# Whole-array products of a fused attention and MLP kernel issued as four products of 32 columns, with one scheduling policy for the whole run

## The chip, the cores and the metric

The kernel runs on one core of one Trainium2 chip. The metric is the device time of one execution, in microseconds (us). The core has a matrix engine (PE, with its weight loads shown apart as PEld), a vector engine (DVE), a scalar engine that evaluates functions (ACT), a general engine (POOL) and a queue engine (SP) that issues most transfers. PE writes its products to PSUM, a memory of 8 banks of 128 partitions by 512 numbers; only ACT and DVE read it here.

## What is computed

A block of 2048 tokens of width 512 goes through a layer norm, and then through two branches that are added to the input:

```
xn = layernorm(x)
A  = softmax(q k^T / 4) v, 32 heads of width 16, then @ wo      (q, k, v = xn @ wqkv)
h  = layernorm(xn)
u  = gelu(h^T @ w1 + b1)        512 x 1376
y  = (u @ w2 + b2)^T            2048 x 512
out = x + A + y
```

The attention is the bulk: 32 heads of 2048 x 2048 scores, each score exponentiated once. All inputs and the output are bfloat16.

## The kernel before

**Blocks and groups.** The scores are cut in 32 blocks (4 blocks of 512 queries times 8 sets of 4 heads), and each block in 16 groups of 128 keys: 512 groups. A group holds 4 heads, and so 4 products K*Q of 32 rows each (line 663; a head's width of 16 is padded to 32), one for each quarter of the rows of the array. Each gives 128 keys by 512 queries in one PSUM bank.

**Two ways to exponentiate.** A group goes either to ACT or to DVE. On ACT (line 686), two instructions take two banks each (128x1024). On DVE, four first passes (line 746, or 754 for two banks at once) turn the scores into 16-bit integers whose bits are read as bfloat16, a rough exponential; two more "planes" are made from the result by adding a constant (line 759 on DVE, line 766 on POOL), and the three planes together approximate the exponential. So a group given to ACT costs four P*V products, one given to DVE twelve.

**P*V.** Line 699 multiplies the exponentials with V. Four products stand side by side, each with 128 rows and 32 columns of the array (16 columns of V, a column of ones for the denominator, padding), and each writes 32 partitions of the same PSUM bank, number 6. These four are called a quad below.

**Whole-array products.** Everything else on PE uses all 128 rows and columns in one product: the transposes of the normalised input (line 781), the projections to Q, K and V (line 604), the two products of the MLP (lines 1016 and 1047), the output projection (lines 1057 and 1065), sums that are carried through the identity (line 1095), and fillers of zeros (lines 826 and 1797). Transposes and part of the projections have 128 moving columns, the others 512. They accumulate in banks 4, 5 and 7.

**Who sets the order.** All instructions are laid out by a planner inside the kernel when it is built (class Sched, line 170 on, and the functions from line 1300 on). It keeps a clock for each engine, adds each instruction with a duration (`occ`) and a delay to its result (`lat`), and at each step asks for PE (pe_step, line 1724, and pe_fill, line 1649), DVE (dve_step, line 1846), POOL and SP (misc_step, line 1904) what to issue next. On PE it chooses between scores for ACT, scores for DVE, P*V and whole-array products. It knows three forms of the array, called S (scores), P (P*V) and F (whole array), and charges SWITCH = 95 ns (line 166) when the form changes. The choice between ACT and DVE for a group falls out of this, as does every queue's order; once built, each engine runs its list in order and waits on semaphores.

**Policies.** Sixteen numbers steer the choices: how long to wait for scores, how to rank P*V against whole-array products, when DVE takes groups, and so on. POLICY (line 97) holds 66 such tuples, one for each 10 us of the planned time, and line 1940 changes to the next.

**Denominators.** At a block's end its result is copied from PSUM, the denominators are gathered through DRAM by SP's transfers, inverted on DVE (line 1283), broadcast by four transfers, and multiplied in on POOL (line 1305). LAT_I and LAT_B (line 445) are the delays that the planner assumes for the second gathering and the broadcast.

**Constants.** The function late_consts (line 515) sets up the output weights and b1h (line 526), the bias of the MLP in single precision, a cast of 128x11 numbers that is read when the first MLP product is evacuated (line 1027).

Of the kernel before, what the change touches and what calls it, by code (L numbers as in the profile page):

```python
# [15 lines left out]
S = 2048  # L16
# [3 lines left out]
F = 1376  # L20
# [46 lines left out]
class Op:  # L67
# [29 lines left out]
POLICY = [  # L97
    (160.0, 150.0, 400.0, -1, 0, 1300.0, 0.0, 0.05, 2, 3, 2, 7500.0, 0, 0.0, 1000.0, 1),
    (115.0, 150.0, 300.0, -1, 0, 900.0, 100.0, 0.05, 2, 5, 2, 8000.0, 84539, 150.0, 1000.0, 1),
    (135.0, 160.0, 250.0, -1, 0, 1300.0, 0.0, 0.0, 3, 2, 2, 7500.0, 73548, 0.0, 1000.0, 1),  # L100
    (135.0, 160.0, 250.0, -1, 0, 1300.0, 0.0, 0.0, 3, 2, 2, 7500.0, 73548, 0.0, 1000.0, 1),
    (135.0, 160.0, 250.0, -1, 0, 1300.0, 0.0, 0.0, 3, 2, 2, 7500.0, 73548, 0.0, 1000.0, 1),
    (180.0, 80.0, 400.0, -1, 0, 1300.0, 0.0, 0.1, 2, 3, 2, 5500.0, 43264, 0.0, 700.0, 2),
    (160.0, 150.0, 400.0, -1, 0, 1300.0, 0.0, 0.05, 2, 3, 2, 7500.0, 0, 0.0, 1000.0, 1),
    (240.0, 150.0, 500.0, -1, 1, 1300.0, 0.0, 0.05, 1, 4, 0.9, 5500.0, 84839, 0.0, 1000.0, 1),
    (225.0, 140.0, 400.0, 1, 1, 1300.0, 200.0, 0.05, 1, 5, 2, 8500.0, 76820, 0.0, 800.0, 1),
    (205.0, 160.0, 350.0, -1, 0, 900.0, 0.0, 0.05, 1, 3, 2, 8500.0, 36251, 0.0, 800.0, 1),
    (130.0, 80.0, 200.0, -1, 0, 900.0, 100.0, 0.2, 2, 3, 2, 10500.0, 47584, 0.0, 900.0, 0),
    (140.0, 70.0, 400.0, 1, 1, 2000.0, 0.0, 0.05, 3, 5, 2, 8500.0, 0, 0.0, 1100.0, 1),
    (230.0, 70.0, 400.0, 1, 0, 900.0, 0.0, 0.05, 3, 5, 2, 8000.0, 41963, 1.0, 700.0, 1),  # L110
    (160.0, 150.0, 400.0, -1, 0, 1300.0, 0.0, 0.05, 2, 3, 2, 7500.0, 0, 0.0, 1000.0, 1),
    (160.0, 150.0, 400.0, -1, 0, 1300.0, 0.0, 0.05, 2, 3, 2, 7500.0, 0, 0.0, 1000.0, 1),
    (210.0, 120.0, 550.0, -1, 0, 1300.0, 0.0, 0.05, 2, 3, 0.9, 8000.0, 0, 0.0, 1000.0, 1),
    (180.0, 210.0, 550.0, 1, 0, 900.0, 100.0, 0.05, 1, 5, 2, 10500.0, 0, 0.0, 1100.0, 1),
    (160.0, 190.0, 400.0, 1, 0, 2000.0, 0.0, 0.1, 1, 2, 2, 5500.0, 0, 150.0, 1100.0, 0),
    (230.0, 170.0, 500.0, 1, 1, 2000.0, 100.0, 0.0, 1, 3, 2, 7500.0, 34273, 150.0, 1000.0, 2),
    (230.0, 140.0, 350.0, -1, 0, 1300.0, 0.0, 0.1, 3, 5, 2, 7500.0, 64300, 0.0, 1100.0, 2),
    (230.0, 140.0, 350.0, -1, 0, 1300.0, 0.0, 0.1, 3, 5, 2, 7500.0, 64300, 0.0, 1100.0, 2),
    (160.0, 150.0, 400.0, -1, 0, 1300.0, 0.0, 0.05, 2, 3, 2, 7500.0, 0, 0.0, 1000.0, 1),
    (125.0, 120.0, 500.0, 1, 1, 900.0, 0.0, 0.2, 3, 4, 0.9, 8500.0, 53346, 0.0, 800.0, 1),  # L120
    (125.0, 120.0, 500.0, 1, 1, 900.0, 0.0, 0.2, 3, 4, 0.9, 8500.0, 53346, 0.0, 800.0, 1),
    (225.0, 150.0, 300.0, -1, 0, 1300.0, 200.0, 0.1, 2, 4, 0.9, 10500.0, 77244, 0.0, 1100.0, 1),
    (165.0, 200.0, 550.0, -1, 1, 1300.0, 0.0, 0.1, 2, 4, 2, 7000.0, 7520, 0.0, 1200.0, 1),
    (160.0, 150.0, 400.0, -1, 0, 1300.0, 0.0, 0.05, 2, 3, 2, 7500.0, 0, 0.0, 1000.0, 1),
    (160.0, 150.0, 400.0, -1, 0, 1300.0, 0.0, 0.05, 2, 3, 2, 7500.0, 0, 0.0, 1000.0, 1),
    (120.0, 140.0, 550.0, -1, 0, 1300.0, 0.0, 0.1, 3, 3, 2, 5500.0, 0, 0.0, 1000.0, 0),
    (120.0, 140.0, 550.0, -1, 0, 1300.0, 0.0, 0.1, 3, 3, 2, 5500.0, 0, 0.0, 1000.0, 0),
    (235.0, 90.0, 550.0, 1, 1, 1300.0, 100.0, 0.05, 3, 3, 0.9, 8000.0, 37810, 0.0, 1100.0, 0),
    (120.0, 240.0, 350.0, -1, 0, 2000.0, 0.0, 0.05, 2, 4, 2, 10500.0, 56289, 0.0, 500.0, 1),
    (160.0, 100.0, 550.0, -1, 1, 2000.0, 0.0, 0.2, 3, 5, 2, 9500.0, 62766, 0.0, 500.0, 0),  # L130
    (130.0, 210.0, 200.0, -1, 0, 1300.0, 0.0, 0.05, 2, 3, 2, 5500.0, 42813, 1.0, 700.0, 1),
    (130.0, 210.0, 200.0, -1, 0, 1300.0, 0.0, 0.05, 2, 3, 2, 5500.0, 42813, 1.0, 700.0, 1),
    (185.0, 110.0, 550.0, -1, 0, 2000.0, 0.0, 0.2, 2, 4, 2, 8000.0, 0, 0.0, 700.0, 1),
    (145.0, 90.0, 300.0, 1, 0, 1300.0, 100.0, 0.05, 2, 2, 0.9, 7000.0, 71587, 0.0, 900.0, 1),
    (175.0, 190.0, 450.0, -1, 0, 2000.0, 200.0, 0.0, 1, 3, 2, 7500.0, 15056, 0.0, 500.0, 2),
    (130.0, 160.0, 400.0, -1, 0, 1300.0, 0.0, 0.05, 2, 5, 0.9, 7000.0, 0, 0.0, 1100.0, 1),
    (180.0, 190.0, 450.0, 1, 0, 1300.0, 0.0, 0.0, 1, 2, 2, 7500.0, 49636, 0.0, 1000.0, 1),
    (205.0, 230.0, 300.0, -1, 0, 1300.0, 200.0, 0.1, 1, 2, 2, 10500.0, 0, 0.0, 1000.0, 2),
    (160.0, 150.0, 400.0, -1, 0, 1300.0, 0.0, 0.05, 2, 3, 2, 7500.0, 0, 0.0, 1000.0, 1),
    (125.0, 140.0, 400.0, -1, 1, 1300.0, 0.0, 0.2, 2, 3, 2, 9500.0, 77989, 0.0, 500.0, 2),  # L140
    (205.0, 180.0, 200.0, -1, 1, 1300.0, 100.0, 0.05, 2, 5, 2, 7500.0, 0, 1.0, 1800.0, 1),
    (170.0, 120.0, 350.0, -1, 0, 1300.0, 0.0, 0.05, 1, 3, 2, 7500.0, 96514, 0.0, 900.0, 2),
    (215.0, 190.0, 250.0, -1, 1, 900.0, 0.0, 0.2, 3, 5, 2, 5500.0, 0, 1.0, 1400.0, 2),
    (120.0, 100.0, 400.0, 1, 0, 1300.0, 200.0, 0.2, 1, 3, 0.9, 10500.0, 26863, 0.0, 500.0, 1),
    (180.0, 240.0, 400.0, -1, 0, 2000.0, 200.0, 0.05, 2, 2, 2, 8500.0, 81850, 0.0, 1800.0, 2),
    (195.0, 140.0, 300.0, 1, 1, 1300.0, 100.0, 0.05, 3, 5, 0.9, 6500.0, 0, 1.0, 1800.0, 0),
    (110.0, 70.0, 500.0, -1, 0, 1300.0, 0.0, 0.2, 2, 3, 2, 7500.0, 0, 0.0, 1100.0, 0),
    (190.0, 230.0, 400.0, -1, 1, 2000.0, 0.0, 0.1, 2, 3, 2, 7000.0, 97277, 0.0, 1400.0, 1),
    (115.0, 120.0, 550.0, -1, 0, 900.0, 100.0, 0.0, 3, 3, 2, 8000.0, 76554, 0.0, 1400.0, 1),
    (145.0, 80.0, 450.0, -1, 0, 900.0, 0.0, 0.05, 3, 3, 2, 7500.0, 0, 0.0, 700.0, 1),  # L150
    (115.0, 190.0, 350.0, -1, 0, 900.0, 0.0, 0.1, 2, 3, 2, 8000.0, 14865, 1.0, 1100.0, 1),
    (140.0, 60.0, 400.0, -1, 0, 900.0, 100.0, 0.0, 1, 5, 0.9, 7500.0, 65796, 150.0, 1000.0, 0),
    (185.0, 220.0, 500.0, 1, 0, 2000.0, 100.0, 0.1, 2, 2, 0.9, 7500.0, 0, 0.0, 500.0, 1),
    (115.0, 180.0, 550.0, -1, 0, 1300.0, 0.0, 0.05, 3, 5, 2, 9500.0, 57145, 150.0, 1000.0, 0),
    (115.0, 230.0, 350.0, -1, 1, 1300.0, 100.0, 0.0, 2, 4, 2, 5500.0, 49062, 0.0, 900.0, 2),
# [185 lines left out]
def bass_parallel_sum__softmax_full_mha__mixer_token_mlp__prompt_kernel(  # L341
# [18 lines left out]
    with ExitStack() as es:  # L360
# [81 lines left out]

        NPRE = 4
        TABLE = 1283.0
        LAT_I, LAT_B = 3500.0, 3000.0


        sc.add("pool", lambda e: e.memset(ident[:], 0.0), writes=[("ident",)], occ=200, lat=430)
# [1647 lines left out]
```

## Time and profile before

| what | us |
|---|---|
| median of 3 runs | 665.76 (663.84 to 665.94) |
| profiled execution | 664.15 |
| its span, first to last instruction | 662.4 |
| PE busy / weight loads busy | 650.1 / 191.4 |
| ACT busy | 648.7 |
| DVE busy | 614.1 |
| POOL busy | 416.2 |
| mean granted clock of PE | 0.996 |

Busy time of PE and ACT counts an instruction from its start to its (modelled) end, and instructions of one engine overlap, so a busy engine may still wait a little. The prices in the text that follows are therefore taken from the start of one instruction to the start of the next. A line with "x4" in a timeline stands for four instructions merged, with the time from the start of the first to the end of the last. "Idle before, releaser" is time in which an engine did nothing, and what ended it. The chain of work that ended last is followed back from the last instruction: at each step to what released it, or to the instruction before it on its engine.

### The profile page before, as it was taken

The numbers are of one execution on the slowest core, as the hardware profiler recorded it, in microseconds if no ns is written. First come the engines' busy times: TensorE is split into PE (matmuls) and PEld (weight loads), VectorE is DVE, ScalarE is ACT, GpSimd is POOL, SyncE is SP. The second block draws the span as 40 slices with busy tenths as digits, with TensorE's granted clock in tenths as the row PEclk, the third lists the DMA queues.
The fourth block names the chain that finished last, engine by engine and source line by source line (L and its number), as shares of the span: only waits on it lengthen the run. The fifth ranks groups of instructions, "written<-read, shape, count | busy, mean of one in ns | idle before, by whom it ended". The sixth has DMA issues, their size and how long they took to land.

```text
span 662.4 us, 15718 instructions
## 1 busy us (share of the span) xinstructions
PE 650.1 (98%) x6387; PEld 191.4 (29%) x6387; DVE 614.1 (93%) x1059; ACT 648.7 (98%) x709; POOL 416.2 (63%) x287
## 2 busy tenths in 40 slices
PE   8999999999999999999999999999999999999997
PEld 4533333322222222222222222222222222222222
DVE  7888999999999999999998999999999998989995
ACT  7989999999999999999999999999999999999996
POOL 5640585664754664665768667697578657596731
PEclk9989999999999999999999999999999999999999
DMA  7025100022022222220012211212110221312011
GB/s 223 2 65 93 35 14 19 23 57 52 15 49 61 52 54 57 50 39 18 22 38 58 74 49 43 64 46 64 34 43 20 52 55 35 89 50 51 26 31 49
DMA packets 78368, 32.67 MB, mean 49 GB/s; under 512 B 63004, under 2 KB 74204, under 8 KB 78296
## 3 DMA queue, kind: packets, MB, share of 16 engines
q1 hardware_dynamic: 77864, 31.27, 19.3%
q8 instruction: 50, 0.82, 0.5%
q10 hardware_dynamic: 432, 0.39, 0.2%
q14 instruction: 22, 0.18, 0.1%
HBM read 26.08 MB, written 2.61 MB: 43 GB/s over the span
## 4 chain that ended last, share of the span: by engine, by line
PE 72%; ACT 21%; DVE 4%; DMA 1%; SPq 1%; POOL 0%; issue 0%; DVEq 0%; POOLq 0%
PE ps L663 26%; PE ps L699 26%; ACT pT L686 21%; PE ps L1016 7%; PE ps L604 6%; PE ps L1047 5%; PE ps L1057 2%; SPq L435 1%; PE ps L781 1%; DMA den_s<-den_scr 0%; DVE plx L746 0%; DVE wqkv_sb L746 0%; DMA x_sb<-in_A_x_dram 0%; DVE h_sb L590 0%; ACT QT L624 0%
## 5 line engine op out<-in xcount | busy, mean ns | idle before, releaser
L686 ACT ACTIVATE pT<-ps 128x1024 bf16<-128x1024 f32 x685 | 630.4, 1133 | 3.2 <-PE ps L663 3.0
L663 PE MATMUL ps<-QT,KT 32*128 32x512 bf16 x2048 | 279.4, 385 | 4.9 <-ACT pT L686 2.9
L663 PEld LDWEIGHTS ps<-QT,KT 32*128 32x128 bf16 x2048 | 71.5, 91 | 269.2 <-ACT pT L686 247.6
L699 PE MATMUL ps<-pT,V 128*32 128x512 bf16 x1370 | 129.4, 390 | 0.3 <-DVE OT L1268 0.3
L746 DVE TENSOR_SCALAR x_sb<-ps 128x512 int16<-128x512 f32 x174 | 115.5, 684 | 7.1 <-PE ps L663 6.2
L746 DVE TENSOR_SCALAR xn_sb<-ps 128x512 int16<-128x512 f32 x156 | 102.5, 683 | 6.2 <-PE ps L663 5.5
L746 DVE TENSOR_SCALAR plx<-ps 128x512 int16<-128x512 f32 x106 | 70.2, 684 | 7.6 <-PE ps L663 6.8
L746 DVE TENSOR_SCALAR wqkv_sb<-ps 128x512 int16<-128x512 f32 x78 | 51.3, 684 | 3.9 <-PE ps L663 3.5
L1016 PE MATMUL ps<-h_sb,w1blk 128*128 128x512 bf16 (+1 forms) x176 | 54.0, 386 | 0.0
L1047 PE MATMUL ps<-gT,w2blk 128*128 128x512 bf16 (+1 forms) x176 | 53.7, 385 | 0.0
L699 PEld LDWEIGHTS ps<-pT,V 128*32 128x32 bf16 x1370 | 32.2, 94 | 67.5 <-issue 63.5
L746 DVE TENSOR_SCALAR xnT<-ps 128x512 int16<-128x512 f32 x64 | 41.9, 682 | 1.9 <-PE ps L663 1.5
L604 PE MATMUL ps<-xnT,wqkv_sb 128*128 128x512 bf16 (+1 forms) x188 | 40.9, 316 | 0.3
L766 POOL TENSOR_TENSOR plx<-xn_sb,shift_w 128x1024 int32<-128x1024 int32 x12 | 22.7, 1891 | 25.4 <-DVE x_sb L759 20.7
L766 POOL TENSOR_TENSOR xn_sb<-x_sb,shift_w 128x1024 int32<-128x1024 int32 x15 | 28.3, 1891 | 15.4 <-DVE xn_sb L759 7.3
L699 PE MATMUL ps<-x_sb,V 128*32 128x512 bf16 x372 | 36.1, 382 | 0.2 <-DVE OT L1268 0.2
L766 POOL TENSOR_TENSOR x_sb<-plx,shift_w 128x1024 int32<-128x1024 int32 x13 | 24.5, 1891 | 13.4 <-DVE x_sb L759 12.1
L746 DVE TENSOR_SCALAR w1blk<-ps 128x512 int16<-128x512 f32 x46 | 30.6, 684 | 1.8 <-PE ps L663 1.3
L766 POOL TENSOR_TENSOR x_sb<-xn_sb,shift_w 128x1024 int32<-128x1024 int32 x12 | 22.7, 1891 | 14.4 <-DVE xnT L759 8.2
L699 PE MATMUL ps<-xn_sb,V 128*32 128x512 bf16 x318 | 30.5, 382 | 0.0
L1305 POOL TENSOR_TENSOR oT<-OT,denb 128x512 bf16<-128x512 f32 x16 | 20.3, 1271 | 14.6 <-DMA denb<-rec_scr 9.2
L1305 POOL TENSOR_TENSOR otmp<-OT,denb 128x512 bf16<-128x512 f32 x15 | 19.1, 1271 | 16.3 <-DVE x_sb L759 10.8
(190 smaller groups left out, 857.9 us busy)
## 6 DMA issues: line engine op xcount, KB each, us to landing
denb<-rec_scr SPq DMA_DIRECT2D x124, 64.0 KB, 2.0
w1blk<-in_B_w_dram SPq DMA_DIRECT2D x10, 512.0 KB, 5.3
w2blk<-in_B_w_dram SPq DMA_DIRECT2D x16, 320.0 KB, 3.7
xres<-in_A_x_dram SPq DMA_DIRECT2D x16, 128.0 KB, 2.2
QT<-qst SPq DMA_DIRECT2D x120, 16.0 KB, 1.8
out_dram<-osb SPq DMA_DIRECT2D x14, 128.0 KB, 1.7
wqkv_sb<-in_A_wqkv_dram SPq DMA_DIRECT2D x3, 384.0 KB, 8.8
x_sb<-in_A_x_dram SPq DMA_DIRECT2D x2, 512.0 KB, 7.8
```

Source lines behind the costliest of these rows:

```text
L435: return eng.dma_start(dst, src)
L604: return sc.add("pe", lambda e: e.matmul(dst, lhsT=lhsT, rhs=rhs, start=(ct == 0), stop=(ct == NCT - 1)), reads=reads, writes=[("bank", bk ...
L663: return sc.add("pe", lambda e: e.matmul(bank(bk), lhsT=KT[32 * r:32 * r + 32, T, 128 * kt:128 * (kt + 1)], rhs=QT[32 * r:32 * r + 32, slo ...
L686: return sc.add("act", lambda e: e.activation(pT_buf(buf), ps[:, slot * 1024:(slot + 1) * 1024], ACTF.Exp, scale=EXP_SCALE), reads=[("bank ...
L699: return sc.add("pe", lambda e: e.matmul(bank(PV_BANK)[32 * r:32 * r + 32, :], lhsT=vt_[:, off:off + 32], rhs=rhs, start=start, stop=stop, ...
L746: return sc.add("dve", lambda e: e.tensor_scalar(plane_i[pb][:, 512 * r:512 * (r + 1)], bank(bk), BIAS, 0.0, ALU.add, ALU.max), reads=[("b ...
L766: return sc.add("pool", lambda e: e.tensor_tensor(plane_w[pb], plane_w[pb0], shift_w[:, j:j + 1].broadcast_to([128, 1024]), ALU.add), read ...
L781: op = sc.add("pe", lambda e, ct=ct: e.transpose(ps_bf[:, bk * 1024 + half * 512 + ct * 128: bk * 1024 + half * 512 + (ct + 1) * 128], xn_ ...
L1016: op = sc.add("pe", lambda e: e.matmul(bank(xb)[0:m, :], lhsT=w1blk[:, slot, st, 0:m], rhs=h_sb[:, st, :], start=(st == 0), stop=(st == NT ...
L1047: op = sc.add("pe", lambda e: e.matmul(bank(xb), lhsT=w2blk[0:m, slot, ft, :], rhs=gT[0:m, ft, :], start=first, stop=last), reads=([("w2bl ...
L1057: return sc.add("pe", lambda e: e.matmul(bank(bk), lhsT=oT[:, par, T, 128 * sti:128 * (sti + 1)], rhs=wo_c[:, T, :], start=first, stop=las ...
L1305: op = sc.add("pool", lambda e: e.tensor_tensor(dst, OT32[:, eb, :], denb[:, :], ALU.mult), reads=[("OT32", eb)] + [("denb", r) for r in r ...
```

## The change

Every whole-array product of the main loop goes through a new function `mm`, which issues it as four products of 32 columns each, with 128 rows, one beside the other; each writes 32 partitions of the same bank. A flag, `quad`, is off during the opening (which is laid out by hand) and on from the start of the planner's loop. The planner gives the four the form P, so that a change of form is now only between S and P; its tests for form F become tests for S. In the same edit the 66 policies become one; LAT_I goes from 3500 to 4300 and LAT_B from 3000 to 3100; the cast b1h moves from DVE to POOL; and the measure of PE's recent activity that decides on fillers counts the new products by their size.

```
-POLICY = [
-    (160.0, 150.0, 400.0, -1, 0, 1300.0, 0.0, 0.05, 2, 3, 2, 7500.0, 0, 0.0, 1000.0, 1),
...
-]
+POLICY = [(130.0, 150.0, 300.0, -1, 0, 1300.0, 0.0, 0.05, 2, 3, 2, 7500.0, 0, 0.0, 1000.0, 2)]
...
-        LAT_I, LAT_B = 3500.0, 3000.0
+        LAT_I, LAT_B = 4300.0, 3100.0
...
-            sc.add("dve", lambda e: e.tensor_copy(b1h[:], b1c_bf[:]), reads=[("b1c",), ("b1c2",)],
-                   writes=[("b1h",)], occ=80)
+            sc.add("pool", lambda e: e.tensor_copy(b1h[:], b1c_bf[:]), reads=[("b1c",), ("b1c2",)],
+                   writes=[("b1h",)], occ=120, lat=230)
...
+        quad = [False]
+
+        def mm(dst, lhsT, rhs, start, stop, reads, writes, n=512, m=128, turn=False):
+            lat = 430.0 if n == 512 else 265.0
+            occ = 226.0 if n == 512 else 56.0
+
+            def form(e, a, b, pos):
+                if turn:
+                    return e.transpose(dst[a:b, :], lhsT[:, a:b], rhs, **pos)
+                return e.matmul(dst[a:b, :], lhsT=lhsT[:, a:b], rhs=rhs, start=start, stop=stop, **pos)
+            if not quad[0]:
+                return sc.add("pe", lambda e: form(e, 0, m, {}), reads=reads, writes=writes, occ=occ, lat=lat, cfg="F")
+            for a in range(0, m, 32):
+                op = sc.add("pe", lambda e, a=a: form(e, a, min(a + 32, m), dict(tile_position=(0, a))),
+                            reads=reads, writes=writes, name="q5" if n == 512 else "q1",
+                            occ=(4.0 if a + 32 < m else occ - 12.0), lat=lat + 10.0, cfg="P")
+            return op
+
         def proj_mm(dst, lhsT, rhs, ct, reads, bk, n=512):
-            return sc.add("pe", lambda e: e.matmul(dst, lhsT=lhsT, rhs=rhs, start=(ct == 0), stop=(ct == NCT - 1)),
-                          reads=reads, writes=[("bank", bk)], occ=(226 if n == 512 else 56),
-                          lat=(430 if n == 512 else 265), cfg="F")
+            return mm(dst, lhsT, rhs, ct == 0, ct == NCT - 1, reads, [("bank", bk)], n)
...
-                same = 0 if c[0] == sc.cfg else 1
+                same = 0 if sc.cfg != "S" else 1
...
-                if same_cfg and c[0] != sc.cfg:
+                if same_cfg and sc.cfg == "S":
                     continue
-                d = 226 + (SWITCH if c[0] != sc.cfg else 0.0)
+                d = 226 + (SWITCH if sc.cfg == "S" else 0.0)
...
-                z.append((o.start, 0.25 if o.name in ("sc", "pv") else (0.25 if o.occ < 100 else 1.0)))
+                z.append((o.start, 1.0 if o.name == "" and o.occ > 200.0 else 0.0625 if o.name == "q1" else 0.25))
...
+        quad[0] = True
         sc.free["sp"] = 0.0
```

The transposes, the MLP products, the output projection, the sums through the identity and the fillers of the main loop call `mm` in the same way as proj_mm does. Because the planner decides every order when the kernel is built, all five engines' lists differ between the two kernels, not only PE's.

## The prediction

> **What bounds the kernel now.** I read the page first: busy shares, then the chain of work that ended last.
>
> ```profile
> PE 650.1 (98%) x6387; PEld 191.4 (29%) x6387; DVE 614.1 (93%) x1059; ACT 648.7 (98%) x709; POOL 416.2 (63%) x287
> ...
> PE 72%; ACT 21%; DVE 4%; DMA 1%; SPq 1%; POOL 0%; issue 0%; DVEq 0%; POOLq 0%
> ...
> L686 ACT ACTIVATE pT<-ps 128x1024 bf16<-128x1024 f32 x685 | 630.4, 1133 | 3.2 <-PE ps L663 3.0
> ...
> L746 DVE TENSOR_SCALAR x_sb<-ps 128x512 int16<-128x512 f32 x174 | 115.5, 684 | 7.1 <-PE ps L663 6.2
> ```
>
> Three engines are nearly full at once. ACT's work is one instruction, the exponential of a 128x1024 tile of scores: 685 in this row and five more that write xn_sb. They overlap (1133 ns each, 690 in some 636 us), so the price of one is a pitch, not a duration. The stretches between the two ends show where ACT is not full:
>
> ```profile
> 42.00:52.00 10.00, 8.87 (x70) 3.01 (x70) 8.21 (x16) 7.37 (x8) 3.70 (x2) 0.83 0.66 153
> 52.00:439.00 387.00, 386.21 (x3794) 110.56 (x3792) 365.22 (x608) 386.92 (x419) 241.87 (x136) 1.00 0.19 44
> 439.00:450.00 11.00, 10.32 (x115) 2.80 (x112) 9.97 (x18) 10.52 (x12) 11.00 (x7) 1.00 0.13 33
> 450.00:655.00 205.00, 201.91 (x2019) 54.32 (x2016) 192.66 (x315) 204.94 (x224) 135.93 (x79) 1.00 0.18 45
> ```
>
> The columns are busy PE, weight loads, DVE, ACT, POOL, then the granted clock. From 52 to 439 and from 450 to 655 ACT is idle for 0.14 us in all. It loses 2.63 us in 42 to 52 and 0.48 us in 439 to 450. The chain in order of time names both places, and gives the pitch:
>
> ```profile
> 42.25 1.63 DVE b1h L526
> ...
> 47.00 1.39 PE ps L604 x9
> ...
> 439.90 3.29 DMA den_s<-den_scr
> ...
> 449.51 67.94 ACT pT L686 x74
> ...
> 589.24 52.35 ACT pT L686 x57
> ```
>
> The 1.63 us is a cast of 128x11 numbers on DVE; the evacuations behind it come late, PE idles, and the granted clock falls to 0.57 in 46 to 50. The last two rows are exponentials back to back: 67.94/74 and 52.35/57, both 0.918 us each. PE's timeline gives its prices, from start to start:
>
> ```profile
> 39.67 0.40 PE L699 MATMUL ps<-pT,V 128*32 128x512 bf16 x4
> 40.00 0.40 PE L604 MATMUL ps<-wqkv_sb,xnT 128*128 128x128 bf16 x4
> 40.33 0.39 PE L663 MATMUL ps<-QT,KT 32*128 32x512 bf16 x3
> ...
> 60.10 0.40 PE L699 MATMUL ps<-pT,V 128*32 128x512 bf16 x4
> 60.33 0.39 PE L699 MATMUL ps<-x_sb,V 128*32 128x512 bf16 x4
> 60.66 0.39 PE L663 MATMUL ps<-QT,KT 32*128 32x512 bf16 x3
> 60.98 0.61 PE L604 MATMUL ps<-xnT,wqkv_sb 128*128 128x512 bf16 x2
> 61.52 0.39 PE L663 MATMUL ps<-QT,KT 32*128 32x512 bf16 x2
> ```
>
> Four P*V products (a quad) or one whole-array product of 512 columns take 0.216 us; the second quad starts 0.23 after the first. Each change of form costs more: scores to anything 0.32 - 0.216 = 0.104; P*V to scores 0.56 - 0.432 = 0.12 (0.116 over all such pairs); whole array to scores 0.54 - 0.432 = 0.108; P*V to whole array 0.33 - 0.216 = 0.116; back 0.104.
>
> **The change, part by part.** Counts are from the instruction orders of the two programs.
>
> *Split between ACT and DVE.* The one policy gives DVE 165 groups of scores in place of 167: ACT gets 694 exponentials for 690. ACT has nothing free in 592 of its 662 us, so this lies on the path: 4 x 0.918 = +3.7 us. DVE's first passes go from 668 to 660 (-8 x 0.684 = -5.5 us), its plane sums from 147 to 155 (+8 x 0.69 = +5.5), POOL's from 187 to 175 (-12 x 1.89 = -22.7); neither pays at the end, since ACT is the one without a gap.
>
> *The cast b1h moves to POOL.* On DVE it took 1.63 us and ACT's loss around it is 2.63. On POOL it follows a memset and precedes plane sums, and its first reader (L1027) starts at 144.4; at its worst it costs what DVE's row shows, 1.63, on an engine idle for 246 us. Gain between 0 (DVE stumbles there over another step) and 2.6; I take -2.6, as no other single DVE step in the chain near it is longer than 0.7.
>
> *LAT_I 3500 to 4300, LAT_B 3000 to 3100.* No instruction changes; the planner places the reciprocal, the broadcast on SP's queue and the multiplication on POOL later. Waits of DVE on den_s are 1.1 us in two places, and ACT's idle time around the larger is 0.48. Gain between 0 and 0.5; I take -0.5. SP's queue then holds back the loads and stores behind the later broadcast; ACT and PE wait for none of those in the views of before.
>
> *PE's changes of form.* Before: scores to P*V 417, back 393, whole array to scores 298, back 274, P*V to whole array 49, back 25. Sum (417+274+25) x 0.104 + (393+49) x 0.116 + 298 x 0.108 = 158.0 us. After: 684 x 0.104 + 683 x 0.116 + 0.1 = 150.5. Seven fewer bursts of scores save 1.5; eight more 512-column products (23 to 35 fillers of zeros among them) less four quads cost 0.9. PE's order gets 8.1 us shorter, of some 632. At the end: bounded by -8.1 (all of it) and 0. I take 0, because the pitch in the pure ACT rows of the chain, 0.918, is the mean pitch elsewhere as well (205 us hold some 223 exponentials): where PE is late by the chain, ACT still loses nothing that shows.
>
> *512-column products as quads.* 551 quads at the 0.216 us that P*V quads show: nothing added. Their four weight loads must hide as those of P*V do:
>
> ```profile
> 302.30 0.11 PEld L1016 LDWEIGHTS ps<-h_sb,w1blk 128*128 128x128 bf16 x2 [0.23 <-issue]
> ...
> 308.62 0.16 PEld L1016 LDWEIGHTS ps<-h_sb,w1blk 128*96 128x96 bf16 x2 [0.23 <-DVE plx L746]
> ...
> 439.18 0.10 PEld L699 LDWEIGHTS ps<-xnT,V17b 128*32 128x32 bf16 x4 [0.23 <-issue]
> ...
> 439.19 0.11 PEld L699 LDWEIGHTS ps<-plx,V 128*32 128x32 bf16 x4
> ```
>
> Two loads of 128 columns start 0.01 us apart (0.11 less one of 0.10), two of 96 columns 0.04 apart (0.16 less 0.12), and the four loads of the next quad start 0.01 after those of the first, 0.2 us before they are needed. By the Trainium skill's page TensorEngine Tiling (Array Packing), Restrictions, column tiling disables Fast Weight Load. The 96-column row agrees that there is a slow way to load; by a slow load that did not hide, 0.03 us on each of 551 quads would make the sum 17 us longer, and the P*V rows, which already load 32 columns, say zero.
>
> *128-column products as quads.* 360 quads in the first 125 us (up to the 123rd exponential) (transposes, K, Q and V projections) in place of 360 single products, some 832 narrow products in the first 45 us alone. The trace has no such quad. Floor: 0.056 us, what the single products show (40.00 to 40.33 is 4 x 0.056 + 0.108). Nearest row: 32-column loads follow each other by 0.016 us, so four in a row, not in parallel, would be 0.064. Ceiling: each narrow product at the pace of a 128-column one, 4 x 0.056 = 0.222. PE's order is full there, so the difference goes to the end: 0 at the floor, 360 x 0.008 = +2.9 at 0.064, 360 x 0.166 = +60 at the ceiling. I take 0.056 (nearest: second quads of P*V lose nothing to loads), 0; both ends stay for the range.
>
> *The tail* keeps its chain (last P*V, two transposes, normalising, four projections, stores); its products become quads at the same price: 0.
>
> **Sum.** 664.15 + 3.7 - 2.6 - 0.5 = 664.75 us for the profiled execution (span 662.4 and 1.75 around it). That execution lies 1.6 below the median shown, 665.76, so I forecast 666.4 for a median: no difference that a measurement tells. (About 0.3%, 2 us, is what these times can tell from no change.)
>
> **The rivals.**
>
> *Faster: the lighter order of PE is felt by ACT.* The pitch could fall from 0.918 to what five exponentials in a row show in ACT's timeline at 299.74, (4.78 - 1.13)/4 = 0.912, or lower. For it: the chain is 72% PE's, so ACT is often released by scores just in time. Against it: the pure ACT rows. Price: 694 x 0.006 = -4.2, bounded by -8.1; time 662.2, down to 658.3. It is faster from 1.9 us off the forecast's 0.6 on.
>
> *Slower: narrow quads cannot be issued fast enough.* The place is the first 125 us. Before never holds a denser run than 24 products in 1.34 us (the 128-column ones, 0.056 each), and over 128 products 0.075; after would need some 0.039 over the first 1150. For it: PE is full there and a late score goes straight to ACT. Against it: P*V quads start four products within 0.01 us. Price per quad above 0.056: 0.36 us per ns; from 62 ns on (+2.2) it decides. At 0.080 it would be +8.6 (675.0), halfway between floor and ceiling, at 0.139, +30 (696). The Trainium skill's page TensorE: Matmul & The Clock Gate, in the section "Wait — 56ns, not 53.3ns?", has a floor of about 25 ns from start to start however small the product; by that an estimate is 0.1 us a quad, +15.8, 682. The four P*V products of a quad start within 0.01 us, so no floor of that kind shows in short bursts; over long ones no run here shows it.
>
> *Slower: one order for all stretches stumbles.* The 66 policies are replaced by one; if the new order has one DVE stumble like b1h's, with the clock dropping behind it, or keeps the loss in 42 to 52, the 3.7 stays and 2.6 come on top: 670 to 672. It decides when one stall of over 1.5 us stands in ACT's row.
>
> *The change doesn't do what it says* (P*V and the new quads still cost a change of form between them, 0.116): the order has 141 places where they meet within a run, 141 x 0.116 = +16.4, 683. Against: second P*V quads with other weights follow at 0.216.
>
> **How the numbers follow.** Cancelling out as summed 0.38 (its own range 663 to 669); lighter order felt 0.24; narrow quads slow 0.20; stumble 0.15; form changes between quads 0.03. Faster: 0.22 of the second and 0.05 of the first, 0.27. Same: 0.27 of the first, 0.02 each of the second and the stumble, 0.31. Slower: the rest, 0.42. The range leaves out what is below 659 (a third of the second, 0.07) and above 678 (half of the narrow quads and all of the last, 0.13): 659 to 678.
>
> **What would show it.** Right: 695 ACT instructions at L638 (694 and the table load) at a mean pitch near 0.918; no idle ACT around 42 to 52 and a granted clock of 1.00 there; second quads 0.22 after the first whichever product they are; 128-column quads 0.056 to 0.06 apart. Wrong: narrow quads at 0.08 and more, with ACT idle in the first 125 us behind PE L663; or a pitch clearly under 0.912, with PE's share of the chain fallen.

## The result, and the profile after

The changed kernel takes 668.09 us in the median of 14 runs, against 665.0 for 14 runs of the kernel before: ratio 1.0045, 95% interval 1.0029 to 1.0061. It is slower by 0.45%, some 3.0 us. One of the 14 runs, 677.2 us at a granted clock of 0.984, is left out of the ratio as a slow one; the median without it is 668.01. The forecast was 666.4, no measurable difference, with 659 to 678 as its range.

The page of the kernel after: engines, PE's instruction queue (packets, MB, share of the transfer engines), the chain that ended last, and the two rows that matter. The first line is the instruction queue in the page of the kernel before.

```profile
q8 instruction: 50, 0.82, 0.5%
...
PE 646.3 (97%) x9112; PEld 190.8 (29%) x9112; DVE 613.7 (92%) x1063; ACT 652.2 (98%) x713; POOL 394.3 (59%) x276
...
q8 instruction: 71, 1.16, 0.7%
...
ACT 63%; PE 31%; DVE 3%; DMA 1%; issue 1%; SPq 0%; POOLq 0%; DVEq 0%
...
L638 ACT ACTIVATE pT<-ps 128x1024 bf16<-128x1024 f32 x689 | 634.0, 1122 | 3.1 <-PE ps L615 2.5
...
L651 PE MATMUL ps<-pT,V 128*32 128x512 bf16 x1378 | 133.4, 389 | 2.0 <-issue 1.4
```

PE issues 9112 products in place of 6387 and is busy 3.8 us less. The chain, 72% PE's before, is now 63% ACT's. One entry is new: P*V waited 1.4 us for "issue", which means for nothing that the profile shows. Row q8 is taken for the queue that brings PE its instructions: 71 packets of 16 KB, 50 before. With 9112 products and as many weight loads (6387 before), that is some 256 instructions for each packet in both kernels.

The stretches of the kernel after; columns as in the prediction (PE, weight loads, DVE, ACT, POOL busy, granted clock, transfers):

```profile
11.00:42.00 31.00, 28.93 (x819) 14.86 (x810) 25.02 (x71) 28.38 (x32) 16.07 (x37) 0.94 0.17 43
42.00:52.00 10.00, 10.00 (x223) 3.90 (x211) 9.76 (x21) 9.93 (x12) 2.99 (x3) 1.00 0.27 76
52.00:439.00 387.00, 382.04 (x5271) 108.94 (x5270) 360.55 (x600) 386.74 (x418) 230.65 (x130) 1.00 0.20 47
439.00:450.00 11.00, 10.48 (x137) 2.78 (x138) 10.98 (x20) 11.00 (x13) 7.66 (x5) 1.00 0.12 32
```

and the first of them in the kernel before:

```profile
11.00:42.00 31.00, 30.85 (x322) 15.25 (x319) 27.09 (x74) 31.00 (x35) 17.06 (x39) 1.00 0.18 48
```

The two losses of ACT that the forecast knew are gone: 0.07 us idle in 42 to 52 (2.63 before), none in 439 to 450 (0.48 before). A new one of 2.62 us has come in 11 to 42, with the clock at 0.94 there. Its place in the timeline of the kernel after:

```profile
15.58 0.09 PEld L651 LDWEIGHTS ps<-pT,V 128*32 128x32 bf16 x1 [0.23 <-issue]
...
17.06 0.62 PE L651 MATMUL ps<-pT,V 128*32 128x512 bf16 x4 [1.41 <-issue]
17.07 0.10 PEld L651 LDWEIGHTS ps<-pT,V 128*32 128x32 bf16 x3 [1.39 <-issue]
...
19.11 1.02 ACT L638 ACTIVATE pT<-ps 128x1024 bf16<-128x1024 f32 x1 [2.07 <-PE ps L615]
```

PE stops in the middle of a quad, after one of its four weight loads, for 1.4 us; the clock is half from 16.89 to 20.30, and ACT waits 2.07 us. In the packets of q8, PE's first one ran from 14.43 to 15.56.

Measured from start to start of the exponentials, the four more of them cost 3.6 us (693 steps for 689, median 0.904 in both kernels). The long steps of before (2.02, 1.53, 1.93 and 1.26 us from 43.5 on) exceed the median by 3.1 us; they are replaced by two at 16.0 and 19.1 (3.15 and 1.44), which exceed it by 2.8. Over the whole run the excess is nearly the same, 20.9 us before and 20.8 after. Outside the exponentials the tail is 0.4 us longer; its chain now runs through a broadcast of denominators.

### The profile page after: what moved, and what is told of

It is laid out like the page before. It is cut to its first block, busy times and chain, and to the rows that moved or that the text cites. A ratio compares the mean times of both kernels' runs of the same rounds, so it can differ in the third digit from the quotient of the medians.

```text
span 666.4 us, 21149 instructions
## 1 busy us (share of the span) xinstructions
PE 646.3 (97%) x9112; PEld 190.8 (29%) x9112; DVE 613.7 (92%) x1063; ACT 652.2 (98%) x713; POOL 394.3 (59%) x276
## 4 chain that ended last, share of the span: by engine, by line
ACT 63%; PE 31%; DVE 3%; DMA 1%; issue 1%; SPq 0%; POOLq 0%; DVEq 0%
ACT pT L638 61%; PE ps L615 11%; PE ps L651 10%; PE ps L548 9%; ACT gT L987 1%; DVE stats L465 1%; PE ps L547 0%; DMA rec_scr<-den_s 0%; DMA x_sb<-in_A_x_dram 0%; DVE wqkv_sb L698 0%; DVE xnT L698 0%; DVE xn_sb L503 0%; DMA denb<-rec_scr 0%; ACT QT L576 0%; DVE w1blk L698 0%
## 5 line engine op out<-in xcount | busy, mean ns | idle before, releaser
L698 DVE TENSOR_SCALAR x_sb<-ps 128x512 int16<-128x512 f32 x196 | 129.0, 682 | 8.8 <-PE ps L615 7.8
L698 DVE TENSOR_SCALAR xn_sb<-ps 128x512 int16<-128x512 f32 x140 | 91.8, 683 | 8.5 <-PE ps L615 7.3
L698 DVE TENSOR_SCALAR xnT<-ps 128x512 int16<-128x512 f32 x100 | 65.3, 682 | 3.9 <-PE ps L615 3.3
L548 PE MATMUL ps<-h_sb,w1blk 128*32 128x512 bf16 x688 | 55.5, 383 | 0.0
L548 PE MATMUL ps<-gT,w2blk 128*32 128x512 bf16 (+1 forms) x704 | 55.2, 384 | 0.0
L698 DVE TENSOR_SCALAR plx<-ps 128x512 int16<-128x512 f32 x72 | 48.0, 685 | 3.9 <-PE ps L615 3.5
L548 PE MATMUL ps<-xnT,wqkv_sb 128*32 128x512 bf16 (+2 forms) x680 | 41.1, 326 | 0.6 <-DVE xnT L534 0.5
L718 POOL TENSOR_TENSOR x_sb<-x_sb,shift_w 128x1024 int32<-128x1024 int32 x11 | 20.8, 1893 | 17.7 <-PE ps L548 5.5
L718 POOL TENSOR_TENSOR plx<-x_sb,shift_w 128x1024 int32<-128x1024 int32 x8 | 15.1, 1893 | 25.6 <-DVE x_sb L711 8.6
L718 POOL TENSOR_TENSOR xn_sb<-x_sb,shift_w 128x1024 int32<-128x1024 int32 x11 | 20.8, 1893 | 14.4 <-DVE wqkv_sb L711 7.4
L718 POOL TENSOR_TENSOR x_sb<-wqkv_sb,shift_w 128x1024 int32<-128x1024 int32 x8 | 15.1, 1893 | 19.5 <-DVE x_sb L711 8.8
```

What stands on the lines that cost most here:

```text
L548: return e.matmul(dst[a:b, :], lhsT=lhsT[:, a:b], rhs=rhs, start=start, stop=stop, **pos)
L698: return sc.add("dve", lambda e: e.tensor_scalar(plane_i[pb][:, 512 * r:512 * (r + 1)], bank(bk), BIAS, 0.0, ALU.add, ALU.max), reads=[("b ...
L718: return sc.add("pool", lambda e: e.tensor_tensor(plane_w[pb], plane_w[pb0], shift_w[:, j:j + 1].broadcast_to([128, 1024]), ALU.add), read ...
```

## The experiments

All ratios are to the kernel before in runs on the same chip. Its median moved between 663.4 and 665.0 from one comparison to another, so kernels of different comparisons are set against each other by ratio (0.001 is 0.66 us), and a distance found so is uncertain by about 1 us.

### 1 and 2: two ways to take the stop at 15.6 us away

Fewer instructions there: products of 128 columns stay whole as long as the planner's clock is under 20 us. The planner is given the same durations, so the order of all engines is that of the change. The traces hold 72 whole products in place of 288 narrow ones, 216 fewer; the expectation, with 54 and 216, took that difference for the number of the narrow ones.

```
+            if quad[0] and n == 128 and sc.free["pe"] < 20000.0:
+                return sc.add("pe", lambda e: form(e, 0, m, {}), reads=reads, writes=writes, name="q1",
+                              occ=occ, lat=lat + 22.0, cfg="P")
```

> The changed kernel with the 128-column products of the first 20 us left whole (54 products, in place of 216 narrow ones); every engine's order is otherwise that of the changed kernel, instruction for instruction. Theory A (PE runs out of instructions: its stream is fetched in packets of 16 KB, 256 instructions, and narrow products use one up four times as fast while the first loads fill the DMA engines): PE's idle time of 1.41 us before P*V at 15.6 us is gone, the pitch of 3.15 us between two exponentials there falls to about 0.92, the clock stays at 1.00, the time falls by 3 us, ratio to before about 1.000. Theory B (the new order itself has a hole there, a wait on DVE or on the load of the inputs): the gap stays within 0.5 us, ratio stays at 1.0045.

Less data in front of the packet: the last 384 columns of each of the three parts of wqkv (three loads of 384 KB each) are issued when nine tiles are normalised, and no longer with the first loads.

```
-        ld_w(1, 1, 4, 16000, "sp")
-        ld_w(2, 1, 4, 18500, "sp")
-        ld_w(0, 1, 4, 21000, "sp")
...
+        def ld_rest():
+            ld_w(1, 1, 4, 6000, "sp")
+            ld_w(2, 1, 4, 7500, "sp")
+            ld_w(0, 1, 4, 9000, "sp")
+        bg.append(Chain("ldw", [Step("sp", ld_rest, gate=lambda: len(ln1_done) >= 9)], -2.0, 0.0))
```

> The changed kernel with the three loads of wqkv's last 384 columns (384 KB each) issued some microseconds later on SP, when nine tiles of the input are normalised; all other orders are those of the changed kernel. If the fetch of PE's instructions is late because it queues behind those loads: the packet that came at 14.43 comes 2 us or more earlier, PE's gap at 15.6 is gone, ratio about 1.000. If narrow products use up instructions faster than a fetch takes even on idle DMA engines: a gap of over 1 us stays, ratio 1.004. If the weights come too late for the first projections of the later heads, a new loss near 35 to 45 us, ratio above 1.005.

The first kernel: 667.72 us, ratio 1.0035 (1.0021 to 1.0049). The second: 665.44, 1.0019 (1.0008 to 1.003). The stop is gone in both. The stretch 11 to 42 of the kernel with the later loads:

```profile
11.00:42.00 31.00, 30.34 (x890) 15.21 (x878) 27.89 (x76) 31.00 (x35) 16.19 (x38) 1.00 0.19 47
```

It holds 890 products at full clock with ACT never idle, more than the kernel after managed in that time (819). So PE can issue narrow quads at this rate; what was missing was the instructions. With the later loads the first packet of q8 runs at 12.44 to 13.92, 2 us earlier. The kernel after stopped behind its 445th product or weight load. There the 446th began 1.50 us after the end of the first packet; with the later loads it came 1.53 us after it, without a stop but hardly in time, and with fewer instructions 6.5 us after it. The later loads are worth 0.0026 in ratio, 1.7 us (2.65 by the medians, and 3.2 by the spans of the two profiled executions, 666.4 and 663.2).

With fewer instructions the gain was 0.0010, 0.7 us, because a new loss stands at 608 us in that profile:

```profile
604.14 0.58 SPq L369 DMA_DIRECT2D xres<-in_A_x_dram  x1
...
608.06 0.69 DVE L1100 TENSOR_TENSOR h_sb<-ps,xres 128x512 f32<-128x512 f32 x1 [2.05 <-DMA xres<-in_A_x_dram]
...
609.41 0.40 PE L618 MATMUL ps<-QT,KT 32*128 32x512 bf16 x1 [1.72 <-DVE xnT L701]
...
611.36 1.02 ACT L641 ACTIVATE pT<-ps 128x1024 bf16<-128x1024 f32 x1 [2.40 <-PE ps L618]
```

DVE waits 2.05 us for rows of x (128 KB, xres) that were asked for 3.9 us earlier; the median from issue to landing in that kernel is 2.1. The first passes behind it come late, then PE's scores, then ACT. A packet of PE's instructions lies in that time, at 605.42 for 1.34 us. The 216 products less had moved all later packets. That the packet delayed the rows is inferred from the times; that the late rows cost 3 us is tested next.

### 3: the rows of x asked for earlier

The first kernel again; after planning, each load of x rows is moved forward in SP's queue by about one output chain, to just behind the sum that frees its buffer. The order of all other instructions stays.

```
+        for o in [z for z in sp if z.name == "ld_xres"]:
+            d = max((rank[id(y)] for y in o.deps), default=None)
...
+            k = min(i, next(j for j, z in enumerate(sp) if rank[id(z)] > d) + 2)
+            if k < i:
+                sc.order.remove(o)
+                sc.order.insert(sc.order.index(sp[k]), o)
+                sp.insert(k, sp.pop(i))
...
```

> This is the kernel with the products of 128 columns left whole before 20 us, in which each load of x rows (xres, 128 KB) is moved forward in SP's queue by about one output chain (9 to 15 us), to just behind the sum that freed its buffer; every other instruction of every engine keeps its place. Theory: its stall at 607.8 us came from one of PE's 16 KB instruction packets that ran beside a load of x rows which the sum waited for. Then the two long pitches of the exponentials there (3576 and 1513 ns against 904) go, 3.3 us with the half clock behind them: first to last exponential 3.0 to 3.3 us less, and the median falls from 667.7 to 664.4 to 665.5 with times that lie closer together. Rival: the order itself stumbles at that place, or the wait goes over to the next load in the queue; then a pitch over 2500 ns stays within 5 us of 608, and the median stays at 667 to 668.

664.66 us, and all 12 runs within 664.56 to 665.24 (665.21 to 668.06 without the move); ratio 1.0004 (0.9994 to 1.0015). The stretch around the loss, first without and then with the move:

```profile
600.00:618.00 18.00, 16.28 (x188) 3.88 (x187) 14.36 (x25) 15.09 (x17) 8.57 (x8) 0.91 0.19 47
```

```profile
600.00:618.00 18.00, 18.00 (x232) 4.81 (x236) 17.31 (x30) 18.00 (x21) 10.30 (x9) 1.00 0.18 43
```

ACT's idle 2.91 us are gone, and the steps of its exponentials sum to 644.2 us, 3.0 less than in the kernel after. Against that kernel the gain is 0.0041, 2.7 us. The packet still stands at 605.42 and DVE no longer waits for rows, so asking earlier cures the loss whether or not the packet caused it. This kernel, with the change's order but neither the stop at 15.6 us nor the late rows, is called the quiet one below.

The same move in the kernel with the later loads:

> The changed kernel with the last 384 columns of wqkv loaded after nine tiles are normalised, and in addition every load of x rows moved forward by one output chain. Theory: the instruction packets meet the x rows in some executions only (in the profiled one of the kernel with the later loads they did not), so the median falls by a little, from 665.4 to 664.5 to 665.2, the profiled span by at most 0.5 us. Rival: the move makes SP's queue wait on DVE or crowds other transfers; then it is 666 or more. If x rows play no part in that kernel at all: 665.4 within 0.4.

665.3 us, 1.0011 (0.9999 to 1.0023): the last case of the expectation, no effect by the median; by the ratios it is 0.5 us, which these times can't tell from none. In the trace without the move DVE waited only 0.3 us for rows.

### 4: the settings and the quads

The change with the 66 settings of before (POLICY as before, all else as after):

> The changed kernel with the 66 settings of before instead of the one (700 exponentials planned against 694). Theory: the settings were found for an order that is gone, so with the quads they are worth no more than any other, and the price of the new order is the number of its exponentials: 668.1 + 6 x 0.917 = 673.6 us, the gap at 15.6 us still there, 672 to 676 with stalls. Rival: the settings have a worth of their own (they keep buffers and PE's work apart in the stretches they were made for); then stalls grow rarer, the excess of the pitches over 0.904 falls from 20.8 us to 17 or less, and the time is 668 to 670.

675.15 us, 1.0161 (1.0131 to 1.0191): as the theory said, 700 exponentials and the stalls on top. Its stop in the opening, in the timeline:

```profile
15.48 0.11 PEld L614 LDWEIGHTS ps<-xnT,wqkv_sb 128*32 128x32 bf16 x5 [0.23 <-issue]
17.09 0.24 PEld L614 LDWEIGHTS ps<-xnT,wqkv_sb 128*32 128x32 bf16 x11 [1.49 <-issue]
```

It is another order, and PE is at another product; yet it stops after 445 products and weight loads, exactly as many as in the kernel after, and goes on 1.49 us after the end of the first packet (14.50 to 15.60), for 1.50. So the place of the stop goes by the count of instructions and its end by the packet, and not by a wait of the program. What PE does in those 1.5 us isn't shown.

And the other way round, everything but the quads: the kernel before with one setting, the new LAT_I and LAT_B, and b1h on POOL.

```
-POLICY = [
...
-]
+POLICY = [(130.0, 150.0, 300.0, -1, 0, 1300.0, 0.0, 0.05, 2, 3, 2, 7500.0, 0, 0.0, 1000.0, 2)]
...
-        LAT_I, LAT_B = 3500.0, 3000.0
+        LAT_I, LAT_B = 4300.0, 3100.0
...
-            sc.add("dve", lambda e: e.tensor_copy(b1h[:], b1c_bf[:]), reads=[("b1c",), ("b1c2",)],
-                   writes=[("b1h",)], occ=80)
+            sc.add("pool", lambda e: e.tensor_copy(b1h[:], b1c_bf[:]), reads=[("b1c",), ("b1c2",)],
+                   writes=[("b1h",)], occ=120, lat=230)
```

> The kernel before with all small edits of the change (one policy, LAT_I and LAT_B, b1h on POOL) but whole-array products: the planner now gives DVE 162 groups and ACT 700 exponentials, against 694 in the changed kernel and 690 before. Theory (the quads' lighter order of PE is paid out as groups that DVE can take): 10 exponentials more than before at 0.918 = +9.2, less 3.1 and 0.9 for the two stumbles = +5.2, ratio 1.008; so quads are worth 5.5 us, of which the gap at 15.6 us takes 3 back. Rival (quads earn nothing, or lose): ratio at or below 1.0045.

680.42 us, 1.0236 (1.0216 to 1.0257), with 700 exponentials. Both cases of the expectation missed (1.008, and 1.0045 or less). Of the 16.6 us by which its profiled span is longer than that of the kernel before, ten exponentials make 9.0, longer steps between them 6.1 and the tail 1.6. ACT waits long at two places, near 535 and 578 us. The longer wait is 4.27 us:

```profile
540.62 1.02 ACT L620 ACTIVATE pT<-ps 128x1024 bf16<-128x1024 f32 x1 [4.27 <-PE ps L597]
```

PE works through it: eleven products of the MLP in a row (536.51 to 539.06) and two sets of four of the output projection stand before the next scores for ACT. So a setting that serves one order of PE was worse with the other, in both directions. What the quads are worth can't be read from kernels that share a setting; each order needs its own.

### 5: the cast, undone in the quiet kernel and done in the kernel before

In the kernel before, the cast on POOL alone (the last four lines of the cut above):

> The kernel before with the cast b1h moved to POOL and nothing else; 690 exponentials and the same order on PE, ACT and SP. The prediction's step: ACT's loss of 2.6 us in 42 to 52 goes, span 659.8, ratio 0.996. Rival (DVE stumbles there over another step, since POOL's long sums hold it up as well): ratio above 0.9985, a stall of over 1.5 us stays between 42 and 52.

663.85 us, 0.999 (0.9974 to 1.0006). The long steps at 43 to 50 us are gone from its trace, 2.4 us of excess in all, but the median gained a quarter of that. The expectation has neither: the time is that of its rival, without the rival's stall. One reason is in the granted clocks. The half clock of 3.41 us in the profiled execution of the kernel before brings its mean to 0.996; of the 120 runs of that kernel beside the experiments, 47 have 0.998 or more and so can't hold it, with a median of 663.26 us, against 664.64 for the 65 at 0.994 to 0.997. In the quiet kernel, the cast back on DVE at its place:

> The quiet kernel of the rows loaded early (664.66 us, no pitch over 1.3 us but the gelu's), with one thing undone: the cast of the bias (b1h) runs on DVE again, at its place in the order, and every other instruction of every engine keeps its place. Theory: the cast alone caused the four long pitches of before at 43 to 50 us (there it took 1629 ns on DVE, with 3.1 us of lost pitch and half clock behind it); then 664.66 + 2.6 to 3.1 = 667.3 to 667.8 us, with half clock for 3.4 us between 42 and 52. Rival: the cast is a stumble in some executions only, or only in the order of before (in the kernel before with the cast on POOL the median gained 0.6 us, not 2.6); then 664.7 to 665.5 and pitches under 1.3 us.

665.02 us, 1.0008 (0.9992 to 1.0023): the rival's time, 0.3 to 0.4 us more than the quiet kernel, which is within the uncertainty (its trace, of a run of 665.70, has steps of 1.48 and 1.41 us where the rival had none over 1.3). The cast's own time differs too. Its row in the kernel before with POOL's row beside it, and then both in the quiet kernel with the cast on DVE:

```profile
42.25 1.63 DVE L526 CAST b1h<-b1c_bf 128x11 f32<-128x11 bf16 x1
...
41.96 3.74 POOL L766 TENSOR_TENSOR x_sb<-plx,shift_w 128x1024 int32<-128x1024 int32 x2
```

```profile
43.69 1.04 DVE L460 CAST b1h<-b1c_bf 128x11 f32<-128x11 bf16 x1
...
41.92 1.89 POOL L721 TENSOR_TENSOR x_sb<-plx,shift_w 128x1024 int32<-128x1024 int32 x1 [6.56 <-DVE plx L701]
43.75 0.95 POOL L450 MEMSET wo_pad<- 128x1024 bf16 x1
```

In both, the cast of 11 numbers a row begins inside a plane sum of POOL and ends with a POOL instruction: at 43.88 with the first of two plane sums (41.96 + 1.87 = 43.83), at 44.73 with the memset behind the sum (44.70). On POOL the cast took 0.25 us. That its price on DVE is what POOL happens to be doing fits both rows; no run moved POOL's work away from it.

### 6: how low each form goes

Settings were looked for with the change's order of PE, by the end that the planner itself gives, in the quiet kernel. Two results, found apart, each with 692 exponentials:

> The quiet kernel of the rows loaded early (quads of 512 columns, products of 128 columns whole before 20 us, x rows loaded one chain ahead, b1h on POOL), with settings that were looked for with this order of PE: 22 different ones over the 66 stretches in place of one; 692 exponentials planned in place of 694, and the planner's own end 2.93 us earlier. Theory: with the collisions gone the order's planned end is what counts, so 664.66 - 2.9 = 661.8 us (661.2 to 662.6), 0.4% under the kernel before, at a spread of under 1 us. Rival: a new order has new collisions of transfers and new stumbles of DVE, as the order of before and that of the change had theirs; then pitches of over 1.4 us stand in ACT's row and it is 663.5 to 667.

> The same with another set of settings, found apart from the first (31 different ones over the stretches, delays of 3700 and 3050 for the denominators): 692 exponentials, planned end 2.48 us earlier than that of the quiet kernel. Theory: 664.66 - 2.5 = 662.2 us (661.6 to 663.0). Rival, as for the other: stalls of its own, 663.5 to 667. If one of the two keeps its planned gain and the other not, the planned end is right to within the luck of one or two stalls.

663.18 us, 0.9986 (0.997 to 1.0001), and 663.28 us, 0.9981 (0.9968 to 0.9994). About half of the planned gain is kept: both times lie above the theory's range and below the rival's. The first has stalls of its own (steps of 1.30 and 1.51 us at 504, 1.43 at 613), as its rival said. The second has none over 1.21 us but the gelu's, so there the planner's end itself promised too much: its steps sum to 1.5 us less than the quiet kernel's, the 1.8 of two exponentials less small delays, and its span falls by 1.3.

For the other side, the kernel before with the cast on POOL and the x rows early:

> The kernel before with the bias's cast on POOL (whole-array products, 66 settings, 690 exponentials; 663.85 us alone) and with every load of x rows moved forward by about one output chain, all else in place. Theory: late x rows need PE's longer instruction stream (71 packets of 16 KB against 50) or its place in time, and in this order no sum waits for x rows in the traces; so the move does nothing: 663.9 within 0.6, with the same spread of some 4 us. Rival: x rows come late in some executions of any order, and that is the spread of before too; then the spread falls to under 1.5 us and the median to 662.0 to 663.0, and the quiet orders of the quads (664.66, 663.28) are slower than a quiet order of whole products.

662.52 us, 0.9974 (0.9958 to 0.999): the median as the rival said, the spread as the theory did, 661.14 to 666.19, nine times up to 662.97 and three from 665.29. The profiled execution is one of the three. DVE in it, and its stretch from 438 to 458:

```profile
440.62 0.25 DVE L1283 RECIPROCAL den_s<-den_s 128x16 f32<-128x16 f32 x1 [0.86 <-DMA den_s<-den_scr]
```

```profile
438.00:458.00 20.00, 19.44 (x150) 4.13 (x142) 14.52 (x25) 16.04 (x18) 13.18 (x8) 0.74 0.09 24
```

This is the wait that the forecast priced at 0.5 us. The gathering of den_s was issued at 437.31, behind eight transfers of QT that hold SP's queue from 432.01 on. Here ACT loses 3.96 us behind a wait of 0.86 us, with PE at half clock from 444.62 to 454.86. The three long times have mean clocks of 0.991 and 0.992, the nine others 0.997 to 0.999, so the long half clock goes with the long times. That the wait starts it is tested next. Three reciprocals (the 3rd, 17th and 20th) are moved back by two DVE instructions in that kernel:

```
+        recs = [z for z in dv if z.name == "rec"]
+        for n in (2, 16, 19):
+            i = dv.index(recs[n])
+            dv.insert(i + 2, dv.pop(i))
...
```

> The kernel before with the cast on POOL and the x rows early (662.52 us; its times lie in two groups, 661.1 to 663.0 and 665.3 to 666.2, and its profiled execution, of the slower group, loses 3.9 us between 444 and 455 behind the reciprocal of the 20th block, which held DVE for 0.86 us until its numbers came); now three reciprocals (the 3rd, 17th and 20th) stand two DVE instructions later, and every other instruction of every engine keeps its order. Theory: the wait of the reciprocal is what tips the stretch in some executions, so the slower group goes: 661.3 us (661.0 to 662.3) with all times under 663.5, 0.5% under the kernel before; the forecast's term for the denominators, 0.5 us, was then a mean over executions of 0 and of 4. And the quiet order of whole products with 690 exponentials is 2.0 us shorter than the quiet order of quads with 692 (663.28): 1.8 of it the two exponentials. Rival: other places tip the run just as well, or the later transfers of the denominators do; then the slower group stays.

660.34 us (six runs, 660.29 to 661.68), 0.9952 (0.9937 to 0.9967): the fastest of all, 0.5% under the kernel before. None of the long times is among them; three of twelve were before, and six without one would come by chance about one time in six, so it isn't sure that they are gone. Its stretch, and its exponentials:

```profile
438.00:458.00 20.00, 19.00 (x190) 5.13 (x187) 18.86 (x33) 20.00 (x23) 16.59 (x11) 1.00 0.21 54
```

```profile
L686 ACT ACTIVATE pT<-ps 128x1024 bf16<-128x1024 f32 x685 | 629.8, 1141 | 0.1
```

ACT waits 0.1 us in the whole run before these 685. Quiet against quiet, then: whole products with 690 exponentials 0.9952, quads with 692 at 0.9981, quads with 694 at 1.0004. The distances are 0.0029, 1.9 us for two exponentials (1.83 at 0.917 each), and 0.0052, 3.5 us for four (3.67); by the medians they are 2.9 and 4.3, by the profiled spans 3.0 and 4.3, of which 0.9 and 0.6 are longer steps in the kernels with quads. Nothing beyond the uncertainty of about 1 us is left that the form of PE's products adds or saves. Whether quads allow fewer than 690 isn't shown: these kernels differ in their settings too, and both with quads keep the early products whole.

## Why the prediction was right in its range and wrong in a term

The time lies inside the range, 1.7 us above the forecast. But the difference is clear of noise, where the forecast said that none would be told; its own chances gave most to slower, 0.42. It lacked one term, the supply of PE's instructions, and two others missed in opposite directions.

**Four more exponentials, +3.7.** Right. The kernel after starts 694, and the chain's pure rows give 0.917 us each:

```profile
127.89 186.24 ACT pT L638 x203
```

The quiet kernels lie 3.5 us apart for four exponentials, with other differences between them.

**The cast, -2.6.** Right for the profiled execution (ACT loses 0.07 us in 42 to 52, full clock), wrong as a price. In the quiet order it is 0.3 to 0.4 us, and in the kernel before 0.6 in the median. "No other single DVE step in the chain near it is longer than 0.7" was true, but the cast met a plane sum of POOL there, and the half clock behind it is not in all runs; which of the two made the stall dear isn't shown.

**The wait for den_s, -0.5.** The stall at 439 to 450 is gone as forecast, though no run changes the two delays alone, and the size was that of one execution. In the traces of the kernels with the order of before, ACT loses 0.48 us there in one and 3.96 in another: moving the reciprocals back brought the ratio from 0.9974 to 0.9952, 1.5 us, and none of the long times occurred in six runs.

**PE's order 8.1 us shorter, taken as 0.** The 8.1 counts one saving twice: the seven fewer bursts of scores are already in the counts of changes (691 changes out of scores before, 684 after), so its own rows make 158.0 - 150.5 - 0.9 = 6.6, and the rival's lowest time would be 659.8. The 0 that it took was right. PE's share of the chain fell from 72% to 31%, and the median step of the exponentials stayed at 0.904 us. The chain said that scores arrive just in time; it did not say that ACT would run faster if they arrived sooner. The rival "lighter order felt" falls with it, for this order.

**Quads at the price of single products, 0.** Right for both sizes. Rows of the kernel after:

```profile
42.73 0.63 PE L548 MATMUL ps<-wqkv_sb,xnT 128*32 128x128 bf16 x32
43.29 0.39 PE L615 MATMUL ps<-QT,KT 32*128 32x512 bf16 x3
...
45.36 0.62 PE L548 MATMUL ps<-xnT,wqkv_sb 128*32 128x512 bf16 x8
45.91 0.39 PE L615 MATMUL ps<-QT,KT 32*128 32x512 bf16 x2
```

Less 0.116 for the change to scores, 32 narrow products take 0.444 us, eight quads of 0.0555; eight wide ones take 0.434, two quads of 0.217. The rival "narrow quads cannot be issued fast enough" had the place right, the first 125 us with ACT idle behind PE's scores, and the cause wrong: the rate holds, the supply of instructions did not. A floor of 25 ns from start to start, which the Trainium skill's page TensorE: Matmul & The Clock Gate states in "Wait — 56ns, not 53.3ns?", does not hold for such products here, at 14 ns each over 32 in a row. The rival "form change between quads" falls too: between a quad of P*V and one of 512 columns of another kind the starts lie 0.227 us apart in the median, as between two quads of the same kind.

**What was missing: the step that failed.** More instructions for the same work are more data for the transfer engines: 71 packets for 50. The step "0 for the narrow quads" looked at the rate of issue and at the weight loads, and not at where the instructions come from. PE's first packet came 2 us later than with part of the opening's loads out of its way, and that stop cost 1.7 us by the ratios, 3.1 us in the profiled execution. The two differ in part because the clock does not always fall: seven of the 13 runs behind the ratio have a mean clock of 0.998 or more, where the profiled one, with its half clock of 3.41 us, has 0.997; all twelve with the later loads have 0.998 or more. The case "one order stumbles" had the right form, one stall of over 1.5 us with the clock dropping behind it, and so nearly the right price (2.6 for 3.1); its place and cause were others. Without the stop and the late rows the change's own order takes 664.66 us, 0.2 to 0.3 us over the kernel before, where the sum had said 0.6. That this is so near is luck: of the 3.1 us that the sum took off, the cast was worth 0.3 to 0.6 and the wait for den_s some 1.5. An estimate from the steps by which the kernel before became quiet (0.6 for the cast, 1.1 for the early rows, 1.5 for the reciprocals, each uncertain by 1 us or more) takes off 3.2; with 3.7 for the exponentials and 1.7 for the stop it comes to +2.2, against 3.0 measured.

## What to carry to other kernels

When an edit issues the same work in more instructions, count the instruction packets as transfers: look at what is queued ahead of the first of them in the opening, and ask for data that an in-order engine will wait on a whole chain early. Where one engine has no gaps, as ACT here, the quiet orders ranked by how many instructions that engine got, whatever the chain's shares said; look for a setting that lowers that number before making another engine lighter. A wait of under 1 us in an engine's in-order queue stood ahead of a loss of 0.5 us in one execution here and of 4 us, with the clock at half, in another; so price it over several executions, and try moving the waiting instruction back by two.

## What the runs showed of the hardware

- PE stopped for 1.4 and 1.5 us in two programs with different orders after the same number of its instructions, 445, with "issue" as the only releaser, and went on 1.50 and 1.49 us after the end of their first instruction packet; with the opening's loads moved away, the packet ran 2 us earlier and the stop did not occur.
- Around a stop of PE of 1.4 us (to 17.06) the granted clock was half from 16.89 to 20.30, 3.41 us, as it was in the kernel before from 46.29 to 49.70.
- A cast on DVE of 128x11 numbers took 1.63 and 1.04 us and ended within 0.05 us of a POOL instruction both times. The Trainium skill's page SBUF — State Buffer, in "SBUF: two separate sides", tells of a port pair that DVE and GpSimd hold in turn for a whole instruction. The first row agrees with it: the cast began inside a plane sum and ended with it. In the second the cast outlasted the sum it began in (to 43.81) and ended with the memset; which of the two held it isn't shown.
